# Moving the inverse's remainder products between the two parts of the forward transform, in a fused FFT convolution and expert kernel

## The chip, the cores and the metric

One core of a Trainium2 chip runs the whole kernel. The metric is the device time of one execution in microseconds (us). Engines are called PE (TensorE), DVE (VectorE), ACT (ScalarE), POOL (GpSimd) and SP (SyncE, which here issues DMAs only).

## The reference

A long convolution along the sequence, with a filter that a small network makes, is followed by a mixture of experts with one expert a token:

```
h_filt = (max(pos_emb @ w1, 0) @ w2) * exp(-0.01 * pos)         # 10048 x 128
u = x * v                                                       # 4 x 10048 x 128
y = irfft(rfft(u, 2S) * rfft(h_filt, 2S), 2S)[:, :S]            # along the sequence
xy = x * y
group, expert = first maximum of xy @ w_group, of xy @ w_expert[group]
out[token] = gate * max(xy @ w1[group, expert], 0) @ w2[group, expert]
```

## The kernel before, in words

The sequence is seen as 79 blocks of 128 positions, and each transform of length 2 x 10048 is done in two steps by matrix products: along the blocks (157 points, of which 79 frequencies are kept, real and imaginary), then along the positions within a block. All values are 32-bit.

`conv` makes the filter's spectrum, then runs over the four batches in five rounds, which are called **ways** here (loop `b` at L275). In way b the forward transform of batch b and the inverse of batch b - 1 go together; way 0 has no inverse, way 4 no forward transform. Ways 1, 2 and 3 are the **combined ways**. The first part of a way runs over the 128 channels in 22 tiles (`OUTS`: twenty of 6 channels, two of 4), taken as eleven **pairs**; the second part, the **middle**, runs over the 79 frequencies, multiplies by the filter's spectrum (`middle`, L595, L778 to L782) and transforms back along the positions (`back`, L791), while the tokens of batch b - 1 are routed (`chosen`, L955 and on).

For one pair of a combined way the program has, in this order:

- `turned` (L810, L813 on PE, L815 on ACT): twelve channels of the previous batch's spectrum `z`, and the rest of them in `zr`, are transposed into four PSUM buffers `pt`, and ACT copies each of these to an SBUF tile `tt`. The first copy holds the transposed rest.
- `dft_main`, twice (L462): the forward products of 64 of the block rows, one tile of 6 channels after the other. They use a 64x64 form of PE's array, four of them side by side. Each tile has two accumulators `psa`. Those of the pair's first tile come out of pool `psA` (2 buffers), those of the second out of pool `psT` (4 buffers), from which the `pt` of `turned` come too.
- `dft_rest`, for both tiles at once (L477 with 32 rows, L487 with 16): the forward products of the remaining block rows, added to the four accumulators. Its last four products end all four. `dft_leave` (L505) then copies each accumulator out: the part up to frequency 63 to `z` by ACT, the remainder to `zr` by DVE.
- `inverse_rest` (L825): the inverse's products with the rest of the frequencies, again in the 64x64 form, from `tt` number one into the two accumulators `po` of the pair (pool `psO`, 2 buffers).
- `inverse_blocks`, twice (L846): the inverse's other products, with 128 rows, added to `po`, tile by tile. ACT copies and turns a half of each `po` into `oo` (L855, L856), DVE adds (L860, `yt`) and multiplies by x (L862, `xy`).

On PE, ACT and DVE these instructions stand in the order in which a scheduler put the program's calls; each engine works through its own list and waits, where the next instruction waits. ACT's list for a steady pair is: four z copies (L505), L855, L856, L855, L856, four tt copies (L815).

Pool and buffer of the forward accumulators are chosen here:

```
pool, tag = (self.psT, "pt") if ((d0 + 2) // GI % (2 if b else 3)) else (self.psA, "ps")
pss = [pool.tile([128, GD, 2 * NB], F32, tag=tag, name="psa") for _ in HALVES]
```

Of the kernel before, what the change touches and what calls it, by code (L numbers as in the profile page):

```python
# [141 lines left out]
def columns(wide):  # L142
    return -(-NB // wide) * (wide + 1)


def groups(n, step):
    return [(i, min(step, n - i)) for i in range(0, n, step)]
# [15 lines left out]
class Kernel:  # L163
# [67 lines left out]
    def conv(self, ctx, right):  # L231
        tc, nc, d = self.tc, self.nc, self.d
        cp = ctx.enter_context(tc.tile_pool(name="cconst", bufs=1))
        zp = ctx.enter_context(tc.tile_pool(name="z", bufs=1))
        self.psA = ctx.enter_context(tc.tile_pool(name="psA", bufs=2, space=PSUM, reuse_waits="tile"))
        self.psT = ctx.enter_context(tc.tile_pool(name="psT", bufs=4, space=PSUM, reuse_waits="tile"))
        banks = ctx.enter_context(ExitStack())
        open_bank = lambda name, n: banks.enter_context(
            tc.tile_pool(name=name, bufs=n, space=PSUM, reuse_waits="tile")
        )  # L240
        self.psO = open_bank("psO", 2)
        self.psr = lambda shape, name: self.psL.tile(shape, F32, tag="pl", name=name)
        self.fmr = self.rp.tile([128, 2 * NCG * 20], F32, tag="fmr", name="fmr")
        self.fm = self.fmr[:, : 4 * NB].rearrange("p (h k) -> p h k", h=2)
        self.fr = self.fmr[:, 4 * NB : 12 * NB].rearrange("p (h c k) -> p h c k", h=2, c=2)

        self.z = zp.tile([128, D, KM, 2], F32, name="z")
        self.zr = zp.tile([128, D, 16, 2], F32, name="zr")
        nc.vector.memset(self.zr[:, :, NB - KM :], 0.0)
        ahead = ExitStack()  # L250
        made, folded, self.loads = [], [], []
        first = ExitStack()
        self.hp = first.enter_context(tc.tile_pool(name="head", bufs=NHEAD))
        with ExitStack() as c2:
            self.filter(c2, ahead, folded)
        for j in range(0, len(OUTS), 2):
            self.dft_rest(0, [self.dft_main(*folded[i]) for i in (j, j + 1)])
            while len(folded) < min(len(OUTS), NFIRST + 3 + j // 2, max(NFIRST, j + 2) + NPROD):
                engine = (nc.vector, nc.gpsimd)[len(folded) % 2]
                folded.append(self.fold(*self.product(0, *OUTS[len(folded)], engine), engine))  # L260
                self.load_next(folded)
        first.close()
        folded = []
        bp = ctx.enter_context(tc.tile_pool(name="back", bufs=1))
        self.fi = bp.tile([128, 2, 3, NB], F32, name="fi")
        nc.sync.dma_start(self.fi.rearrange("p h a t -> p (h a t)"), d["c_fi"])


        xyp = ctx.enter_context(tc.tile_pool(name="xy", bufs=1, reuse_waits="tile"))
        inner = ExitStack()  # L270
        self.sp = inner.enter_context(tc.tile_pool(name="stream", bufs=2, reuse_waits="tile"))
        routing, self.scatters = iter(()), []

        self.anchor, self.loose = None, []
        for b in range(self.nbat + 1):  # L275
            last = b == self.nbat
            if last:
                ahead.close()
                inner.close()
                self.sp = ctx.enter_context(tc.tile_pool(name="stream", bufs=2, reuse_waits="tile"))  # L280
                weights = self.first_weights(right)
            if b > 0:
                xy = xyp.tile([128, NB, D], F32, tag="xy", name=f"xy{b - 1}")
            if b == 1:
                self.router_consts()
            for j, (d0, n) in enumerate(OUTS if b else []):
                if j % 2 == 0:
                    tts = self.turned(d0, min(2 * GI, D - d0), last)
                if not last and j % 2 == 0:
                    units = []  # L290
                    for i in range(j, j + 2):
                        self.run_ahead(b, i, made, folded)
                        self.scatter(1)
                        units.append(self.dft_main(*folded[i]))
                    self.dft_rest(b, units)
                if j % 2 == 0:
                    pos = self.inverse_rest(min(2 * GI, D - d0), tts)
                self.inverse_blocks(b - 1, xy, d0, n, tts, pos[j % 2], j % 2)
                if not last:
                    self.scatter(1 + j % 2)  # L300
                if last:
                    next(weights, None)
                    if j == 16:
                        self.scatter(sum(1 for s in self.scatters if s[0] < self.nbat - 2))
                        self.all[0].load(self.rows)
                for _ in range(3 if last else 1):
                    next(routing, None)
                if last:
                    self.scatter(1 + j % 2)
            made, folded = [], []  # L310
            if b > 0:
                rp = self.rp
                banks.close()
                self.psL = open_bank("psL", 2 if last else 1)
                m = NCG + 1
                shape = [128, columns(m - 1) // m, NE, m]
                oh = rp.tile(shape, F32, tag="oh", name="oh")
                en = self.entries.tile([128, NB, 2], F32, tag="en", name="en")
                pos = rp.tile([*shape[:2], m], F32, tag="pos", name="pos")
                cnt = rp.tile([128, NE], F32, tag="cnt", name="cnt")  # L320
                if not last:
                    self.scratch = self.psL.tile([128, 512], F32, tag="work", name="work")
                args = b - 1, xy, oh, en, pos, cnt
                routing = chain(self.chosen(*args), self.ranked(b - 1, *args[2:]))
                stored = 0
                if last:
                    self.identr = self.rows.tile([128, 128], F32R, name="identr")
                    nc.scalar.copy(self.identr, self.ident)
                    for i in range(CHOSEN):
                        if i == 3:  # L330
                            self.all[0].prepare(self.rows, self.psA)
                        next(routing)
            if not last:
                back = []
                for i, (k0, n) in enumerate(groups(NB, 2)):
                    back.append(self.middle(b, k0, n))
                    if len(back) > LAG:
                        self.back(*back.pop(0))
                    if b == 1 and i == 1:
                        self.clear_none()  # L340
                    self.scatter(i % 4 // 3, False)
                    while b > 0 and stored < min(len(groups(NB, 4)), (i + 2) * 20 // STORES):
                        self.store(b - 1, xy, stored)
                        stored += 1
                    next(routing, None)
                for i in range(-AHEAD - 1, 0):
                    self.run_ahead(b + 1, i, made, folded)
                for args in back:
                    self.back(*args)
                for _ in routing:  # L350
                    pass
                if b > 0:
                    banks.close()
                    self.psO = open_bank("psO", 2)
        return routing
# [1383 lines left out]
```

## Time and profile before

| | us |
|---|---|
| runs: median (lowest to highest) | 1792.52 (1791.48 to 1794.69) |
| profiled execution: its time | 1792.42 |
| profiled execution: its span in the trace | 1790.2 |
| PE busy | 1745.2 |
| DVE busy | 1362.4 |
| ACT busy | 1211.5 |
| POOL busy | 1007.6 |

The span is the time from the first to the last instruction of the trace; the 2.2 us to the execution's time lie around it. Busy times are sums over the span. Lines are those of the kernel before. In the trace every 32-bit product shows as two passes of PE, so that the 12 products of L825 in a pair are 24 rows of the trace; a merged row gives their count as x24.

### The profile page before, as it was taken

Reading aid. Unit: us, or ns where it says so; the run is one execution under the profiler, and the core shown is the slowest. Engines: PE = TensorE matmul, PEld = TensorE weight load, DVE = VectorE, ACT = ScalarE, POOL = GpSimd, SP = SyncE. Lnnn points to the kernel's source line nnn. Section 1 sums busy time; section 2 is a strip of 40 time slices with the busy share of each in tenths; the row PEclk is TensorE's granted clock in tenths of the full one; section 3 lists DMA queues with packets and bytes.
Section 4 is the critical chain, followed back from the end, with each engine's and each line's share of the span. In section 5 each row is a group of like instructions: output and inputs, shape, how many; then the busy total and the mean of one; then the engine's idle time right before and its main releaser. Section 6 shows DMA issues by size and latency. Waiting matters only on the chain.

```text
span 1790.2 us, 44965 instructions
## 1 busy us (share of the span) xinstructions
PE 1745.2 (97%) x15302; PEld 1471.2 (82%) x15302; DVE 1362.4 (76%) x3048; ACT 1211.5 (68%) x2624; POOL 1007.6 (56%) x1147
## 2 busy tenths in 40 slices
PE   8999999999999999999999999999999999999998
PEld 7977888878787878777888788888888888889998
DVE  5587777797689768845888898777777777778886
ACT  6573377537654765466777777777777777778886
POOL 4526801577867776784566657766764333333454
PEclk9999999999999999999999999999999999999999
DMA  5697976989898999668633434344443333223342
GB/s 176 224 339 231 306 220 212 324 264 291 290 320 262 288 300 312 222 202 276 210 115 117 126 119 161 126 140 141 138 128 92 92 93 95 88 78 103 96 126 93
DMA packets 201327, 337.30 MB, mean 188 GB/s; under 512 B 26856, under 2 KB 88525, under 8 KB 201088
## 3 DMA queue, kind: packets, MB, share of 16 engines
q1 hardware_dynamic: 170304, 274.57, 48.0%
q0 software_dynamic: 21280, 44.23, 7.0%
q10 hardware_dynamic: 9504, 15.54, 3.0%
q8 instruction: 123, 2.02, 0.5%
q14 instruction: 116, 0.95, 0.2%
HBM read 259.27 MB, written 75.53 MB: 187 GB/s over the span
## 4 chain that ended last, share of the span: by engine, by line
PE 54%; ACT 1%; issue 1%; DVE 1%; DMA 0%; SPq 0%; POOL 0%; DVEq 0%; ACTq 0%; POOLq 0%
PE ph L1550 8%; PE ph L1552 8%; PE py L1572 8%; PE ph L1551 8%; PE py L1570 8%; PE py L1571 8%; PE ptm L1584 2%; PE px L1501 1%; PE po L825 1%; PE po L846 1%; PE ptr L955 0%; ACT oo L856 0%; ACT hh L1558 0%; DMA xo<-x_out 0%; ACT tt L815 0%
## 5 line engine op out<-in xcount | busy, mean ns | idle before, releaser
L1559 DVE SCALAR_TENSOR_TENSOR hl<-ph,hh 128x512 fp32r<-128x512 f32 (+1 forms) x656 | 440.0, 672 | 136.1 <-ACT hh L1558 131.1
L1596 POOL DMA_INDIRECT out<-os,to x320 | 323.4, 1011 | 385.4 <-ACT os L1591 313.0
L1558 ACT ACTIVATE hh<-ph 128x512 fp32r<-128x512 f32 (+1 forms) x656 | 388.8, 593 | 169.1 <-PE ph L1552 139.9
L429 POOL DMA_INDIRECT prow<-stg,adr x316 | 327.5, 1036 | 104.6 <-issue 67.0
L1550 PE MATMUL ph<-xh,wh 128*128 128x512 f32 (+2 forms) x720 | 278.1, 386 | 1.0 <-ACT wh L1529 1.0
L1552 PE MATMUL ph<-xh,wl 128*128 128x512 f32 (+2 forms) x720 | 264.5, 367 | 0.2 <-DVE wl L1539 0.2
L1572 PE MATMUL py<-hh,wl 128*128 128x512 f32 (+2 forms) x720 | 264.3, 367 | 0.0
L1570 PE MATMUL py<-hh,wh 128*128 128x512 f32 (+2 forms) x720 | 264.2, 367 | 0.0
L1551 PE MATMUL ph<-xl,wh 128*128 128x512 f32 (+2 forms) x720 | 263.6, 366 | 0.0
L1571 PE MATMUL py<-hl,wh 128*128 128x512 f32 (+2 forms) x720 | 263.2, 366 | 0.0
L779 POOL TENSOR_TENSOR y<-t 128x256 f32<-128x256 f32 (+1 forms) x160 | 119.5, 747 | 157.8 <-DVE t L778 150.1
L798 ACT COPY z<-pbp 128x512 f32<-128x512 f32 x128 | 75.0, 586 | 140.6 <-PE pbp L791 140.4
L791 PE MATMUL pbp<-y,bp 128*128 128x256 f32 x632 | 161.9, 379 | 3.7 <-POOL y L782 3.6
L595 PE MATMUL psb<-z,bt 128*128 128x256 f32 x640 | 161.2, 380 | 3.4 <-PE psb L595 1.4
L1571 PEld LDWEIGHTS py<-hl,wh 128*128 128x128 f32 x720 | 135.7, 188 | 22.6 <-DVE hl L1559 0.6
L1552 PEld LDWEIGHTS ph<-xh,wl 128*128 128x128 f32 x720 | 135.4, 188 | 22.2 <-DVE wl L1539 0.4
L1572 PEld LDWEIGHTS py<-hh,wl 128*128 128x128 f32 x720 | 135.6, 188 | 21.6
L1570 PEld LDWEIGHTS py<-hh,wh 128*128 128x128 f32 x720 | 135.5, 188 | 21.5
L1550 PEld LDWEIGHTS ph<-xh,wh 128*128 128x128 f32 x720 | 135.5, 188 | 16.7 <-ACT wh L1529 1.2
L1551 PEld LDWEIGHTS ph<-xl,wh 128*128 128x128 f32 x720 | 136.0, 189 | 15.8
L778 DVE TENSOR_TENSOR t<-psb,ht 128x512 f32<-128x512 f32 (+1 forms) x160 | 108.6, 679 | 43.1 <-POOL y L779 13.9
L791 PEld LDWEIGHTS pbp<-y,bp 128*128 128x128 f32 x632 | 117.7, 188 | 25.4 <-POOL y L782 8.0
(270 smaller groups left out, 3367.6 us busy)
## 6 DMA issues: line engine op xcount, KB each, us to landing
ws<-m_w SPq DMA_DIRECT2D x178, 256.0 KB
xv<-xv_in SPq DMA_DIRECT2D x80, 512.0 KB
ht<-hspec SPq DMA_DIRECT2D x156, 256.0 KB
bt<-c_b SPq DMA_DIRECT2D x95, 256.0 KB
bp<-c_bp SPq DMA_DIRECT2D x76, 256.0 KB
xyd<-xy SPq DMA_DIRECT2D x76, 256.0 KB
stg<-xyd SPq DMA_DIRECT2D x76, 256.0 KB
xg<-prow SPq DMA_DIRECT2D x66, 260.0 KB
```

Of the source, the lines that this page charges most:

```text
L429: ins = self.nc.gpsimd.indirect_dma_start(self.d["prow"], bass.IndirectOffsetOnAxis(ap=u.adr[:, t + t // u.wide + 1 : t + t // u.wide + 2] ...
L595: nc.tensor.matmul(ps[:, i].rearrange("p s d -> p d s"), bt[:, i], self.frequency(k0 + i, 1)[:, :, 0], start=True, stop=True,)
L791: nc.tensor.matmul(by_part[:, i], bp[:, i], y[:, i], start=True, stop=True,)
L1550: k.fix(nc.tensor.matmul(ph[:, j], wh, self.xh, start=True, stop=False))
L1551: k.fix(nc.tensor.matmul(ph[:, j], wh, self.xl, start=False, stop=False))
L1552: k.fix(nc.tensor.matmul(ph[:, j], wl, self.xh, start=False, stop=True))
L1558: k.fix(nc.scalar.activation(hh, ph, AF.Relu))
L1559: k.fix(nc.vector.scalar_tensor_tensor(hl, ph, 0.0, hh.bitcast(F32), ALU.max, ALU.subtract))
L1570: k.fix(nc.tensor.matmul(self.py, wh, hh, start=(c == 0), stop=False))
L1571: k.fix(nc.tensor.matmul(self.py, wh, hl, start=False, stop=False))
L1572: k.fix(nc.tensor.matmul(self.py, wl, hh, start=False, stop=(c == NC - 1)))
L1596: ins = k.nc.gpsimd.indirect_dma_start(k.d["out"], bass.IndirectOffsetOnAxis(ap=self.to[:, h : h + 1], axis=0), o, None, bounds_check=k.nt ...
```

## The change

Inside a combined way, `inverse_rest` of a pair is called ahead of `dft_rest` of the same pair.

```
                         units.append(self.dft_main(*folded[i]))
-                    self.dft_rest(b, units)
                 if j % 2 == 0:
                     pos = self.inverse_rest(min(2 * GI, D - d0), tts)
+                    if not last:
+                        self.dft_rest(b, units)
                 self.inverse_blocks(b - 1, xy, d0, n, tts, pos[j % 2], j % 2)
```

The line numbers behind it grow by one (L825 becomes L826, and so on). On PE, a steady pair of way 1 before (psa are the forward accumulators, po the inverse's, pt the transposes):

```order
L810 MATMUL pt<-ident,zr 128x128 x3
L813 MATMUL pt<-ident,z 128x128 x12
L462 MATMUL psa<-fmr,eo 64x158 x24
L477 MATMUL psa<-fmr,eo 64x316 x8
L487 MATMUL psa<-fmr,eo 64x158 x8
L825 MATMUL po<-fi,tt 64x158 x12
L846 MATMUL po<-fi,tt 64x79 x24
```

The same pair on PE in the changed kernel:

```order
L811 MATMUL pt<-ident,zr 128x128 x3
L814 MATMUL pt<-ident,z 128x128 x12
L463 MATMUL psa<-fmr,eo 64x158 x24
L826 MATMUL po<-fi,tt 64x158 x12
L478 MATMUL psa<-fmr,eo 64x316 x8
L488 MATMUL psa<-fmr,eo 64x158 x8
L847 MATMUL po<-fi,tt 64x79 x24
```

The twelve products of `inverse_rest` moved from behind the forward rest to the place right behind the forward main; nothing else moved on PE within a pair. The 33 pairs all change in this way, but for the first of way 3, where five of the twelve already stood ahead of L462.

On ACT, the list of a steady pair in the changed kernel, from the z copies on (its order is that of before, with lines one higher):

```order
L506 COPY z<-psa 128x384 x4
L856 ACTIVATE oo<-po 64x474
L857 COPY oo<-po 64x474
L856 ACTIVATE oo<-po 64x474
L857 COPY oo<-po 64x474
L816 COPY tt<-pt 128x384
L816 COPY tt<-pt 128x512 x3
```

The z copies wait for the end of the forward rest on PE, and L856 and all that follows stand behind them.

On DVE, where way 1 goes over into its middle stage, before (yt and xy are the inverse's last steps, psb the first product of the middle, t its product with the spectrum):

```order
L860 TENSOR_TENSOR yt<-po,oo 128x316
L862 TENSOR_TENSOR xy_3007<-yt,xo 128x79x4
L860 TENSOR_TENSOR yt<-po,oo 128x316
L778 TENSOR_TENSOR t_4587<-psb,ht 128x512
L862 TENSOR_TENSOR xy_3007<-yt,xo 128x79x4
L781 TENSOR_TENSOR t_4590<-psb,ht 128x512
```

And in the changed kernel:

```order
L861 TENSOR_TENSOR yt<-po,oo 128x316
L779 TENSOR_TENSOR t_4587<-psb,ht 128x512
L863 TENSOR_TENSOR xy_3007<-yt,xo 128x79x4
L861 TENSOR_TENSOR yt<-po,oo 128x316
L782 TENSOR_TENSOR t_4590<-psb,ht 128x512
L863 TENSOR_TENSOR xy_3007<-yt,xo 128x79x4
```

The last product of xy, on which the router's transposes wait, now has two spectrum products ahead of it where it had one. POOL's list is the same; on SP some loads of the middle stage (`ht`, `bt`, `bp`) change places with each other and with the stores of `xy`.

## Rows read from the trace of the kernel before

**Rows 1.** The page: busy time by engine, and PE's granted clock in 40 slices

```profile
PE 1745.2 (97%) x15302; PEld 1471.2 (82%) x15302; DVE 1362.4 (76%) x3048; ACT 1211.5 (68%) x2624; POOL 1007.6 (56%) x1147
...
PEclk9999999999999999999999999999999999999999
```

**Rows 2.** Timeline of PE, way 1, first pair: start us, duration us, instructions

```profile
225.72 1.84 PE L462 MATMUL psa<-fmr,eo 64*64 64x158 f32 x48
227.49 0.79 PE L477 MATMUL psa<-fmr,eo 32*64 32x316 f32 x16
228.07 0.47 PE L487 MATMUL psa<-fmr,eo 16*64 16x158 f32 x16
```

**Rows 3.** Timeline of PE, way 1, fourth pair

```profile
247.72 1.91 PE L462 MATMUL psa<-fmr,eo 64*64 64x158 f32 x48
249.56 0.79 PE L477 MATMUL psa<-fmr,eo 32*64 32x316 f32 x16
250.14 0.47 PE L487 MATMUL psa<-fmr,eo 16*64 16x158 f32 x16
250.55 1.04 PE L825 MATMUL po<-fi,tt 64*64 64x158 f32 x24
251.51 1.86 PE L846 MATMUL po<-fi,tt 128*64 128x79 f32 x48
```

**Rows 4.** Timeline of ACT, fourth and fifth pair; in brackets idle time before, and releaser

```profile
247.58 0.97 ACT L815 COPY tt<-pt 128x384 f32<-128x384 f32 x2
...
250.68 1.63 ACT L505 COPY z<-psa 128x384 f32<-128x384 f32 x4 [1.15 <-PE psa L487]
...
252.66 0.56 ACT L855 ACTIVATE oo<-po 64x474 f32<-64x474 f32 x1 [0.36 <-PE po L846]
...
254.96 0.48 ACT L815 COPY tt<-pt 128x384 f32<-128x384 f32 x1
```

**Rows 5.** Timeline of PE: L487 of pair ten (way 1), one and ten (ways 2, 3)

```profile
294.39 0.48 PE L487 MATMUL psa<-fmr,eo 16*64 16x158 f32 x16
...
400.52 0.47 PE L487 MATMUL psa<-fmr,eo 16*64 16x158 f32 x16
...
467.25 0.47 PE L487 MATMUL psa<-fmr,eo 16*64 16x158 f32 x16
...
576.70 0.47 PE L487 MATMUL psa<-fmr,eo 16*64 16x158 f32 x16
...
643.88 0.47 PE L487 MATMUL psa<-fmr,eo 16*64 16x158 f32 x16
```

**Rows 6.** Timeline, end of way 1's pairs and start of its middle stage

```profile
299.21 1.35 ACT L815 COPY tt<-pt 128x256 f32<-128x256 f32 x3
...
300.32 0.79 PE L477 MATMUL psa<-fmr,eo 32*64 32x316 f32 x16
...
301.04 0.77 PE L825 MATMUL po<-fi,tt 64*64 64x158 f32 x16
301.17 1.20 ACT L505 COPY z<-psa 128x256 f32<-128x256 f32 x4 [0.61 <-PE psa L477]
...
301.74 1.32 PE L846 MATMUL po<-fi,tt 128*64 128x79 f32 x32
...
302.55 0.43 ACT L855 ACTIVATE oo<-po 64x316 f32<-64x316 f32 x1 [0.18 <-PE po L846]
...
302.98 2.00 PE L595 MATMUL psb<-z,bt 128*128 128x256 f32 x8
...
303.44 0.49 DVE L860 TENSOR_TENSOR yt<-po,oo 128x316 f32<-128x316 f32 x1 [0.82 <-ACT oo L856]
...
304.77 0.68 DVE L778 TENSOR_TENSOR t<-psb,ht 128x512 f32<-128x512 f32 x1
...
305.90 1.09 PE L955 MATMUL ptr<-ident,xy 128*128 128x128 f32 x8 [0.91 <-DVE xy L862]
```

**Rows 7.** Timeline of PE, way 2, third group of the middle stage's products

```profile
483.95 1.11 PE L595 MATMUL psb<-z,bt 128*128 128x256 f32 x4 [0.78 <-PE psb L595]
```

More of the change, by code (lines that the diff above doesn't have):

```diff
@@ L294, in conv @@
                         units.append(self.dft_main(*folded[i]))
-                    self.dft_rest(b, units)
                 if j % 2 == 0:
                     pos = self.inverse_rest(min(2 * GI, D - d0), tts)
+                    if not last:
+                        self.dft_rest(b, units)
                 self.inverse_blocks(b - 1, xy, d0, n, tts, pos[j % 2], j % 2)
```

## The prediction

> **What bounds the kernel now.** I read the page first: TensorE is busy in 97% of the span, at the upper of its two clock levels in all 40 slices [rows 1]. So what adds a wait on PE adds to the time. The change is in the three combined ways alone (b = 1, 2, 3; eleven tile pairs each), so the next view is the timeline of PE there.
>
> The first pair of way 1 runs with PE alone as its limit: the forward main (L462) takes 225.72 to 227.49, 1.77 us [rows 2]. In a steady pair it takes 247.72 to 249.56, 1.84 us [rows 3]. Something holds PE for 0.07 us, and the rows of ACT in the same stretch show what. ACT ends its second copy of transposed data (L815, two copies from 247.58) at 248.55 [rows 4], about half-way through L462, where the second tile of the pair begins. That tile's two accumulators come out of pool psT, whose four buffers also hold the transposes; by the program's waits its first products wait for the first and second L815 copy of the same pair. PE is at its limit and ACT's chain just reaches it.
>
> The reader should see a ring, each step started by the end of the one before. Second L815 copy ends, to L477: 1.01. L477 to L487: 0.58. L487 to L825: 0.41. L825 to L846: 0.96 [rows 3]. L846's first half to ACT's first L855: 1.15, and that row says that ACT waited 0.36 for L846. L855, L856, L855, L856 and up to L815: 2.30 (252.66 to 254.96). Two L815 copies: 0.97 [rows 4]. Sum 7.38, which is the pair's period (247.58 to 254.96). In the same ring stands a second branch, now idle: L487 releases the z copies (L505), 0.54 after its start, and they keep ACT for 1.63 [rows 3, 4]. They are done at 252.31, 0.35 before L846 lets ACT go on. That 0.35 is what the change spends.
>
> **Part 1: the moved products.** Per pair the same instructions run; L825 now follows L462, which uses the same 64x64 tiles, and L477 follows L825. What does it save? 24 passes of L825 take 0.96 [rows 3], the 16 passes of the last pair 301.04 to 301.74, 0.70 [rows 6]. Eight passes are 0.26, so 24 are 0.79 without the change of tile form around them, and 0.17 goes with entering and leaving the form. One such change falls away: 33 x 0.17 = 5.6 us of PE time. Bounds: nothing saved (L825 still 0.96), or twice the 0.17, if entering and leaving each cost that much.
>
> The Trainium skill (TensorEngine Tiling, Tiling Modes, Key Properties) says that a change of tiling mode, unlike a change of tile, drains TensorE. The trace agrees with 0.17 us; by that rule alone the change is a gain, and this is the first rival below.
>
> **Part 2: what is moved behind it.** The forward rest (L477, L487) starts 0.79 later relative to L462. It completes all four accumulators of the pair, so all four z copies leave 0.79 later. ACT's order of instructions is the same before and after: z copies, then L855, L856 twice, then the L815 copies. The 0.35 of room is used up and the other branch closes the ring: second L815 copy ends, to L477 1.01 + 0.79 = 1.80; to L487 0.58; to the z copies 0.54; z copies 1.63 and 0.02 to the next; L855 to L815 2.30; two copies 0.97. Sum 7.84, against 7.38 now. PE's own work would allow 7.38 - 0.07 - 0.17 = 7.14, so PE gets a stall of 0.70 in the middle of L462 in each pair but the first of a way. The gain of part 1 is off the path: it only lengthens that stall.
>
> L487 of pair 1 to L487 of pair 10 in way 1 is 228.07 to 294.39, 66.32 [rows 2, 5]; nine rounds of 7.84 are 70.56: +4.2. L487 of pair 1 is itself 0.79 late. Bounds of one round: 7.14 (the copies don't hold PE) and 8.0 (L825 costs its full 0.96).
>
> **Part 3: the end of a way.** From L487 of pair 10 to the first transposes for the router (L955) is 294.39 to 305.90, 11.51 [rows 5, 6]. Afterwards: z copies and up to L855 0.54 + 1.63 + 0.02 = 2.19; to the first L815 +2.30 = 4.49; from there to L477 1.11 (299.21 to 300.32), plus L825 at 0.70 - 0.17 = 0.53, gives 6.13; the last z copies start 0.85 later (300.32 to 301.17) and take 1.20: 8.18. The middle stage's first product (L595) now waits for them too, where it was free at 302.98. L855 at 8.20; L860 0.89 later (302.55 to 303.44): 9.09; L860 to L955 2.46. The order on DVE changes here: a second spectrum product (L781) comes ahead of the last product of xy, on which L955 waits. It costs at most the 0.68 of its sister L778; I take 0.5, as L778, moved between L860 and the L862 that needs it, covers some of a wait there. That is 12.05: +0.5. Bounds 0 and 0.9, the wait that L955 has now.
>
> SP's queue also changes its order where the ways hand over (loads of bt, ht and bp against the stores of xy). No row shows PE waiting for one of these; I take 0, between -0.9 and +0.9 a way, again the wait of L955 [rows 6]. POOL's order does not change; its row scatters run in the longer pairs. PE may get back the 0.78 that it waits early in way 2's middle stage [rows 7], since POOL, which is behind there with scatters, has more time.
>
> **Sum.** Way 1: 0.8 + 4.2 + 0.5 = 5.5. Way 2: the same span is 400.52 to 467.25, 66.73 [rows 5], 0.4 longer for a stop of PE within the ring, which stays; 5.5 - 0.8 = 4.7. Way 3: 576.70 to 643.88, 67.18 [rows 5], 0.9 longer; such stops vanish where they fall into the new stall, so I count half as absorbed, and five of the twelve moved products of its first pair already stood ahead of L462: 4.8. Together 15.0. Everything behind is a chain on PE and shifts. The profiled execution took 1792.42, the median is 1792.52: 1792.4 + 15.0 = 1807.4.
>
> **The rivals.** (a) *The form change is all that counts.* If the copies don't hold PE, the 5.6 us come through, less 3 x 0.5 at the ends: 1788.3. For it: PE is busy in 97%, and the 0.17 that a change of form costs shows in every pair. Against it: L462 at 1.84 against 1.77, and a period that equals the ring's sum to 0.01. It decides where the z copies end before L846's first half does: counted from L487 that is 0.54 + 1.63 = 2.17 against 0.41 + 1.15 = 1.56 with L846 right behind it, so the copies would have to take under 1.0. Chance 0.07.
> (b) *No change*, within 3.6 us: PE gets back in the middle stages most of what the pairs lose, as DVE and POOL, and not PE, pace their ends. For it: waits like that of rows 7. Against: one such wait a way, below 1 us each. 1794; chance 0.05.
> (c) *More than the ring*: the order of SP's loads adds a wait at each hand-over, or the new stall brings the clock down. With 0.9 a way twice over 3 ways it is 1813. PE now has waits of 0.9 at upper clock [rows 1, 6], longer than the new 0.70, so I give the clock little. Chance 0.06.
> The Trainium skill (TensorE: Matmul & The Clock Gate, "A second HAM failure mode: psum-queue depth-cycling") reports short idles between groups, from cycling through PSUM buffers, that made the clock swing. At the lower level PE's 2.9 us of the ring would double, some 87 us over 30 pairs; no row here shows such a fall.
>
> **How the numbers follow.** The ring as forecast has 0.82, and 1807.4 is its value. Its own spread: the end of a way 0 to 0.9 and SP's 0.9 either way make about 4 us, the absorbed stops and the wait of rows 7 another 2. Low end 1801, high end 1812.5; (a), (b) and the far part of (c) are left out. 0.2% is 3.6 us, about what a measurement of this kernel tells from no change: faster 0.07, same 0.05, slower 0.88.
>
> **What would show it.** Right: from the second pair of each way L463 (L462 before) lasts about 2.4 us, with PE waiting for tt of L816; periods of 7.84; L826 at 0.79; ACT's wait ahead of L856 gone and that ahead of the z copies longer, near 1.9 instead of 1.15. Wrong: periods of 7.2 (rival a), or L826 still at 0.96 (part 1).

## The result and the profile after

| | before | after |
|---|---|---|
| median (lowest to highest), us | 1792.46 (1791.1 to 1794.69) | 1807.99 (1806.63 to 1810.82) |
| profiled execution's span, us | 1790.2 | 1804.7 |

The ratio is 1.0089, 95% interval [1.0077, 1.0101]: the change costs 15.5 us. The forecast was 1807.4, in 1801.0 to 1812.5.

Some experiments below ran on other chips, on which PE pauses again and again for nothing that the trace shows and the kernel before itself takes some 2047 to 2050 us; their times are compared only with that, and their readings are taken from way 1, whose pairs show no such pauses: the four kernels that ran on both kinds of chip agree in way 1's length within 0.02 us.

The page of the changed kernel, busy time and PE's granted clock:

```profile
PE 1757.7 (97%) x15302; PEld 1474.4 (82%) x15302; DVE 1366.7 (76%) x3048; ACT 1211.7 (67%) x2624; POOL 1008.7 (56%) x1147
...
PEclk9999999999999999998999999999999999999999
```

ACT, DVE and POOL run as many instructions as in [rows 1]. PE's busy time grew by 12.5 us with the same 15302 instructions: while PE waits in a forward main, single passes of L463 run where four run side by side otherwise, and the page counts that time as busy. The one slice with an 8 lies at 812 to 857 us, behind the combined ways. The kernel before was granted the same 0.89 in the stretch that answers to it, 797 to 842; there the fall lies across the border of two slices, and both still show a 9, so the row of nines in [rows 1] hides some 10 us at the lower level. Over the combined ways the granted clock is 1.00 in both kernels, so the clock is no part of the difference.

Timeline of PE, first pair of way 1 in the changed kernel (start, duration, instructions), which answers to [rows 2]:

```profile
225.61 1.84 PE L463 MATMUL psa<-fmr,eo 64*64 64x158 f32 x48
227.27 0.98 PE L826 MATMUL po<-fi,tt 64*64 64x158 f32 x24
228.18 0.79 PE L478 MATMUL psa<-fmr,eo 32*64 32x316 f32 x16
228.77 0.48 PE L488 MATMUL psa<-fmr,eo 16*64 16x158 f32 x16
```

Where nothing holds PE, the new order is the better one: L463 to L826 takes 1.66 where L462 to L477 took 1.77, and L826 to L478 takes 0.91 where L825 to L846 took 0.96 in a steady pair. The first pair as a whole takes 7.14 from its first transpose to the next pair's, against 7.30 before.

The same view, fourth pair, which answers to [rows 3]:

```profile
248.50 2.41 PE L463 MATMUL psa<-fmr,eo 64*64 64x158 f32 x45
250.63 0.29 PE L826 MATMUL po<-fi,tt 64*64 64x158 f32 x1
250.74 0.31 PE L463 MATMUL psa<-fmr,eo 64*64 64x158 f32 x3
250.76 1.09 PE L826 MATMUL po<-fi,tt 64*64 64x158 f32 x23
251.78 0.79 PE L478 MATMUL psa<-fmr,eo 32*64 32x316 f32 x16
252.37 0.48 PE L488 MATMUL psa<-fmr,eo 16*64 16x158 f32 x16
252.77 1.86 PE L847 MATMUL po<-fi,tt 128*64 128x79 f32 x48
```

From L463 to L478 it is 3.28 here and 2.57 in the first pair: 0.71 of waiting, all within L463. PE's weight loads (PEld) there show what is waited for, and the last line, PEld's waits over all three combined ways (us in total, times, longest), shows it as the longest wait in the list, about 0.6 us in each of 30 pairs; the kernel before has no wait of L462 on `tt` in its list:

```profile
249.53 0.19 PEld L463 LDWEIGHTS psa<-fmr,eo 64*64 64x64 f32 x2 [0.29 <-ACT tt L816]
250.02 0.60 PEld L463 LDWEIGHTS psa<-fmr,eo 64*64 64x64 f32 x19 [0.30 <-ACT tt L816]
...
PEld psa L463 <- ACT tt L816: 18.4, 57, 0.8
```

Timeline of ACT there, which answers to [rows 4] (in brackets idle time before, and releaser):

```profile
249.00 0.48 ACT L816 COPY tt<-pt 128x384 f32<-128x384 f32 x1
...
249.38 1.57 ACT L816 COPY tt<-pt 128x512 f32<-128x512 f32 x3
...
252.90 1.63 ACT L506 COPY z<-psa 128x384 f32<-128x384 f32 x4 [1.95 <-PE psa L488]
254.55 0.57 ACT L856 ACTIVATE oo<-po 64x474 f32<-64x474 f32 x1
...
256.85 0.48 ACT L816 COPY tt<-pt 128x384 f32<-128x384 f32 x1
```

The period is 256.85 - 249.00 = 7.85. The bracket has moved: before, ACT waited 1.15 ahead of the z copies and 0.36 more ahead of L855; now it waits 1.95 ahead of the z copies and not at all behind them. The z copies close the ring.

L488 of pair ten (way 1), and of pairs one and ten (ways 2 and 3), which answer to [rows 5]:

```profile
299.46 0.48 PE L488 MATMUL psa<-fmr,eo 16*64 16x158 f32 x16
...
406.72 0.48 PE L488 MATMUL psa<-fmr,eo 16*64 16x158 f32 x16
...
477.41 0.47 PE L488 MATMUL psa<-fmr,eo 16*64 16x158 f32 x16
...
587.01 0.47 PE L488 MATMUL psa<-fmr,eo 16*64 16x158 f32 x16
...
657.71 0.47 PE L488 MATMUL psa<-fmr,eo 16*64 16x158 f32 x16
```

Nine rounds now take 70.69, 70.69 and 70.70 in the three ways, where they took 66.32, 66.73 and 67.18: every pair now goes at the ring's pace, and the short stops of before are gone in it.

End of way 1's pairs and start of its middle stage, PE, ACT and DVE, which answers to [rows 6]:

```profile
304.37 0.63 PE L463 MATMUL psa<-fmr,eo 64*64 64x158 f32 x11 [0.45 <-ACT tt L816]
...
306.44 1.20 ACT L506 COPY z<-psa 128x256 f32<-128x256 f32 x4 [1.15 <-PE psa L478]
...
307.69 2.00 PE L596 MATMUL psb<-z,bt 128*128 128x256 f32 x8
...
308.55 0.49 DVE L861 TENSOR_TENSOR yt<-po,oo 128x316 f32<-128x316 f32 x1 [0.66 <-ACT oo L857]
...
310.35 0.68 DVE L782 TENSOR_TENSOR t<-psb,ht 128x512 f32<-128x512 f32 x1
...
310.94 0.47 DVE L863 TENSOR_TENSOR xy<-yt,xo 128x316 f32<-128x316 f32 x1
...
311.13 0.67 PE L596 MATMUL psb<-z,bt 128*128 128x256 f32 x2 [1.44 <-issue]
...
311.64 1.03 PE L956 MATMUL ptr<-ident,xy 128*128 128x128 f32 x8
```

L782 stands ahead of the last L863 as the order on DVE said, and PE waits 1.44 where it waited 0.91. The profile names no releaser ("issue"); that it is L782, done at 311.03, is read from the times. But then one more product of the middle stage (L596, 0.51 until L956) comes first, so part of that wait is not lost.

Where the 14.5 us of the span lie, from the first transpose row (L810, now L811) of each stretch: the ten rounds up to the last pair grew by 4.21, 3.80 and 3.08 us in ways 1, 2 and 3 (73.63 to 77.84, 74.03 to 77.83, 76.34 to 79.42). From the last pair to the next way's first pair it is +1.30, +0.58 and +1.40 (98.82 to 100.12, 100.30 to 100.88, 99.28 to 100.68). All that lies behind, 1043.91 before, is 1044.15.

### The profile page after: what moved, and what is told of

Its sections match the earlier page's. It is cut to its first block, busy times and chain, and to the rows that moved or that the text cites. A ratio compares the mean times of both kernels' runs of the same rounds, so it can differ in the third digit from the quotient of the medians.

```text
span 1804.7 us, 44966 instructions
## 1 busy us (share of the span) xinstructions
PE 1757.7 (97%) x15302; PEld 1474.4 (82%) x15302; DVE 1366.7 (76%) x3048; ACT 1211.7 (67%) x2624; POOL 1008.7 (56%) x1147
## 4 chain that ended last, share of the span: by engine, by line
PE 54%; ACT 1%; issue 1%; DVE 1%; DMA 0%; POOL 0%; DVEq 0%; SPq 0%; ACTq 0%; POOLq 0%
PE ph L1551 8%; PE ph L1553 8%; PE py L1573 8%; PE ph L1552 8%; PE py L1571 8%; PE py L1572 8%; PE ptm L1585 2%; PE px L1502 1%; PE ptr L956 1%; PE po L826 1%; PE po L847 0%; PE plt L967 0%; ACT oo L857 0%; ACT tt L816 0%; DMA xo<-x_out 0%
## 5 line engine op out<-in xcount | busy, mean ns | idle before, releaser
L596 PE MATMUL psb<-z,bt 128*128 128x256 f32 x640 | 161.9, 381 | 7.2 <-issue 4.3
L596 PEld LDWEIGHTS psb<-z,bt 128*128 128x128 f32 x640 | 115.4, 188 | 28.6 <-issue 6.9
```

Of the source, the lines that this page charges most:

```text
L596: nc.tensor.matmul(ps[:, i].rearrange("p s d -> p d s"), bt[:, i], self.frequency(k0 + i, 1)[:, :, 0], start=True, stop=True,)
```

## The experiments

**The theory**: ACT's copies close the ring; PE's stall is what ACT's list takes too long. **The rival**: PE itself pays for the new order, ACT's waits only follow. They part when ACT's list alone is made longer or shorter. **A second question** is how much belongs to the last pairs. One table holds the readings: the start of the first transpose of pairs 2 and 10 of way 1, an eighth of the difference (the mean period), and the time from the last pair to way 2's first pair.

| kernel | pair 2 | pair 10 | period | last pair to way 2 |
|---|---|---|---|---|
| before | 231.23 | 290.18 | 7.37 | 98.82 |
| after | 230.96 | 293.81 | 7.86 | 100.12 |
| before, small copy more | 233.67 | 294.74 | 7.63 | 99.49 |
| before, two copies more | 232.17 | 294.97 | 7.85 | 99.79 |
| change in last pairs only | 231.33 | 290.27 | 7.37 | 99.50 |
| change but for last pairs | 230.93 | 293.76 | 7.85 | 99.46 |
| before, two copies off ACT | 230.57 | 289.00 | 7.30 | 98.65 |
| change, one copy off ACT | 232.04 | 291.83 | 7.47 | 99.86 |
| change, two copies off ACT | 231.88 | 289.03 | 7.14 | 99.95 |
| the same, last pairs in the old order | 231.01 | 288.15 | 7.14 | 98.67 |

### ACT made slower in the kernel before

The old order on PE is kept; only ACT gets more to do behind the z copies. First a small copy, a repeat of 128 columns:

```diff
         for _, d0, m, pss in units:
             self.dft_leave(b, d0, m, pss)
+        for _ in range(1 if b else 0):
+            ins = nc.scalar.copy(
+                self.z[:, d0 + m : d0 + m + 1].rearrange("p d k s -> p d (k s)"), pss[1][:, :1, : 2 * KM]
+            )
...
```

> The kernel before, with one copy repeated on ACT behind the z copies of each pair of the combined ways: 128 columns of the second tile's second accumulator once more to the same place, about 0.17 us of ACT per pair (from L505's 0.48 for 384 columns and the 0.11 that 128 columns more or fewer change an ACT copy). Ring theory: the z branch has 0.35 of room before L846's first half, so the period stays 7.38 and the time 1792.5, within 1. Rival, ACT's load itself is what counts (every us of ACT in a pair adds to the pair): 33 x 0.17 = 5.6 more, 1798.

Measured: 2048.35 us, ratio 1.0019 [0.9995, 1.0043], which tells nothing on that chip; the period is 7.63. Timeline of ACT:

```profile
261.61 1.63 ACT L512 COPY z<-psa 128x384 f32<-128x384 f32 x4 [1.15 <-PE psa L487]
263.55 0.27 ACT L491 COPY z<-psa 128x128 f32<-128x128 f32 x1 [0.32 <-DVE zr L512]
263.84 0.56 ACT L862 ACTIVATE oo<-po 64x474 f32<-64x474 f32 x1
```

I had missed on the dose: the repeat takes 0.27, not 0.17, and waits 0.32 for DVE's copy of the remainder. From the end of the z copies (261.61 + 1.63) to L862 it is 0.60, 0.58 more than the usual 0.02. The room is 0.35, so 0.23 should come through, 7.38 + 0.23 = 7.61. The expectation failed and the ring holds, but that reading was made afterwards, so the next run is the test. Here the z copies of the second accumulators are made twice:

```diff
+        for _, d0, m, pss in units if b else ():
+            ins = nc.scalar.copy(self.z[:, d0 + m : d0 + 2 * m].rearrange("p d k s -> p d (k s)"), pss[1][:, :m, : 2 * KM])
...
```

> The kernel before, with the z copies of the second accumulator of each tile done twice, 0.37 each, 0.75 us of ACT more behind the z copies of each pair. Ring theory: 0.35 is covered, 0.40 is not; period 7.38 + 0.40 = 7.78 from the second pair on, 9 x 0.41 a way and some 0.4 at its end, 3 x 4.1 = 12 more: 1804.5. Rival, ACT's load counts in full: 33 x 0.75 = 25 more, 1817. Rival, the form of PE's tiles alone sets the pairs: no change, 1792.5.

Measured: 2055.65 us, ratio 1.0040 [1.0015, 1.0066]; period 7.85. From the first z copy to L860 it is now 263.43 - 260.98 = 2.45, where it is 1.63 [rows 4] and the 0.02 to the next instruction:

```profile
260.98 1.63 ACT L510 COPY z<-psa 128x384 f32<-128x384 f32 x4 [1.15 <-PE psa L487]
262.47 0.94 ACT L491 COPY z<-psa 128x384 f32<-128x384 f32 x2
263.43 0.56 ACT L860 ACTIVATE oo<-po 64x474 f32<-64x474 f32 x1
```

That is 0.80 more (0.75 were expected), less the room of 0.35: 0.45, and 7.38 + 0.45 = 7.83, against 7.85; ACT's load in full would have given 8.18. So the old order, with 0.80 us more on ACT, takes the period that the new order takes with its z copies 0.8 later.

### ACT made faster

Two copies of each steady pair go to DVE: the first tt copy and the z copy of the second tile's second accumulator. The same edit goes into the kernel before and into the changed one:

```diff
             if b == 0:
                 copies = (copies[r],) * 2
+            elif r == 1 and (d0 + 2) // GI % 2:
+                copies = (nc.vector.tensor_copy,) * 2
...
-            (nc.vector.tensor_copy if other and len(tts) == 2 else nc.scalar.copy)(tt[:, :m], pt[:, :m])
+            (nc.vector.tensor_copy if (other and len(tts) == 2) or (not other and s is None) else nc.scalar.copy)(tt[:, :m], pt[:, :m])
```

> The kernel before, with two copies of each steady pair taken off ACT and put on DVE: the first tt copy (L815, 128x384) and the z copy of the second tile's second accumulator (L505). Theory (the ring closed by ACT's copies): ACT's chain in the pair gets shorter than PE's own work, so the period of way 1 falls from 7.37 to PE's own 7.30 (its first pair), and nothing below that: 33 x 0.07 = 2 us less, ratio to before 0.999. Rival (the copies do not hold PE; PE pays for the order itself): the period stays at 7.37, ratio 1.000, or above it if the copies on DVE are in the way of its own work.

> The changed kernel with the same two copies on DVE. Theory (ring): ACT no longer closes the ring, the stall in the forward main goes, and the period of way 1 falls from 7.85 to PE's own 7.14 as in the first pair; 30 pairs x 0.71 = 21 us less than the changed kernel, about 1.5 to 4 us below the kernel before with the same two copies (one change of tile form a pair saved, 0.16 each, less what the ends of the ways cost); ratio to before about 0.997. Rival (PE itself pays for the new order): the period stays near 7.85 and the ratio to before at 1.009.

Measured periods: 7.30 and 7.14, both as the theory had them. Both times, 2055.47 and 2056.45, have the ratio 1.0042 ([1.0017, 1.0068] and [1.0016, 1.0068]): on that chip both kernels are slower than the kernel before, and what ways 2 and 3 add there stays open. A steady pair of the changed kernel with the two copies on DVE, from its second run, PE:

```profile
247.74 1.84 PE L463 MATMUL psa<-fmr,eo 64*64 64x158 f32 x48
249.40 0.98 PE L828 MATMUL po<-fi,tt 64*64 64x158 f32 x24
250.32 0.79 PE L478 MATMUL psa<-fmr,eo 32*64 32x316 f32 x16
250.90 0.47 PE L488 MATMUL psa<-fmr,eo 16*64 16x158 f32 x16
251.31 1.86 PE L849 MATMUL po<-fi,tt 128*64 128x79 f32 x48
```

and of the kernel before with them:

```profile
246.66 1.84 PE L462 MATMUL psa<-fmr,eo 64*64 64x158 f32 x48
248.44 0.79 PE L477 MATMUL psa<-fmr,eo 32*64 32x316 f32 x16
249.02 0.48 PE L487 MATMUL psa<-fmr,eo 16*64 16x158 f32 x16
249.42 1.04 PE L827 MATMUL po<-fi,tt 64*64 64x158 f32 x24
250.39 1.86 PE L848 MATMUL po<-fi,tt 128*64 128x79 f32 x48
```

L463 to L849 takes 3.57, L462 to L848 takes 3.73: the 0.16 of one change of form less. In the first the forward main goes through in 1.66, with no stall, although L478 and L488 still come behind L828 and the z copies still leave late. So the new order alone costs PE nothing; it costs what ACT adds. The rival is out.

One copy alone, the first tt copy, on DVE in the changed kernel (the second of the two hunks above):

> The changed kernel with one copy alone on DVE, the first tt copy (L816, 128x384). Theory (ring): 0.4 to 0.5 us come out of the ring, and part of the stall stays: period of way 1 7.40 to 7.50 instead of 7.85, 30 x 0.4 = 12 us less than the changed kernel, ratio to before about 1.002. Rival (PE itself pays): 7.85 and 1.009.

Measured: period 7.47, in the range expected; 2054.36 us, ratio 1.0028 [1.0001, 1.0055]. The dose answers in steps: 7.86 with both copies on ACT, 7.47 with one less, 7.14 with two less, where PE's own work is the limit.

### The last pairs

The change in all pairs but the last of a way, and the reverse:

```diff
+                    if j == 20:
+                        self.dft_rest(b, units)
                 if j % 2 == 0:
                     pos = self.inverse_rest(min(2 * GI, D - d0), tts)
-                    if not last:
+                    if not last and j < 20:
                         self.dft_rest(b, units)
```

> The changed kernel, but the last pair of each combined way keeps the order of before (forward rest, then the inverse's rest), and with it DVE keeps its order at the hand-over. Ring theory: pairs 2 to 10 still take 7.85; at the end of the way 0.6 to 0.7 less than in the changed kernel, so 2 us less, 1806. Rival, most of the loss sits at the hand-overs: the loss falls to a third or less, under 1798.

> The kernel before, with the change in the last pair of each combined way alone. Ring theory: pairs 1 to 10 keep 7.30 to 7.38; at the end of a way the z copies are 0.5 late and DVE has one product more ahead of the last xy, L955 0.5 to 0.9 later, in way 2 won back by the wait that PE has anyway: 1794.5. Rival, most of the loss sits at the hand-overs: 1800 or more.

Measured: 2047.18 (0.9998 [0.9970, 1.0027]) and 2050.55 (1.0009 [0.9984, 1.0033]), both useless as times. In way 1 the first has the ring's period and 0.64 more from the last pair on than the kernel before; the second has the old period and 0.68 more. Together 1.32, against the 1.30 of the whole change: half of the hand-over's loss is the last pair's own order, half is the lateness that the ring has already brought (in the first of the two, PE still waits for `tt` in the last pair's forward main, which takes 2.15 to L480, 302.85 to 305.00, against 1.52 in the kernel before).

> The change in the last pair of each combined way alone, once more for its time over all three ways; in the trace of its first run way 1 was 0.66 us longer than in the kernel before. Theory (the last pair and its hand-over are a small share): 3 x 0.7 = 2 us, 1795, ratio 1.0011. Rival (a third or more of the change's 15.5 us comes from the hand-overs, as way 1's stretch from the last pair to the router's transposes grows by 1.0 to 1.6): 1798 or more, ratio above 1.0025.

Measured: 1793.01 us, ratio 1.0003 [0.9994, 1.0012], so between 1.1 less and 2.2 more than the kernel before. The 2 us of the theory are just inside, the 5 us of the rival are not: the loss is in the pairs.

### Back to whole times

Three kernels of the above, on chips on which the kernel before takes 1793:

> The changed kernel with the two copies on DVE, once more for its time over all three ways. Way 1 took 171.38 us in the trace of its first run, against 172.45 in the kernel before and 177.95 in the changed one. Theory (ring): 3 x 1.07 = 3.2 us less than the kernel before: 1789.3, ratio 0.998; against the changed kernel 18.7 less. Rival (PE itself pays for the new order, and way 1 was an exception): 1800 or more, ratio above 1.004. [...]

> The kernel before with the two copies on DVE, once more for its time over all three ways, as the partner of the changed kernel with the same copies, which took 1791.7 here (1787.9 with the last pairs in the old order). Way 1 took 171.69 us in the trace of its first run, against 172.45 in the kernel before. Theory (ring): without ACT in the way the new order of the ten full pairs is worth 0.16 a pair, so this kernel is about 30 x 0.16 = 5 us above the one with the last pairs old: 1791 to 1793, ratio 0.999 to 1.000. Rival (the gain of that kernel comes from the copies on DVE, and the new order is worth nothing): 1788, ratio 0.997.

Measured: 1791.70 (0.9989 [0.9981, 0.9998]) with the change, 1790.49 (0.9991 [0.9982, 1.0000]) without it. Two copies on DVE take back 16.3 of the changed kernel's us, 1807.99 to 1791.70; 18.7 were expected. With them on DVE the change moves the time by 1.2 us (on two chips, and within the noise of the two ratios), where it cost 15.5. That settles the cause of the loss over all three ways. But the change's gain does not show in these two times: way 1 is 171.40 against 171.70, and way 2 is 174.80 against 173.01.

The remaining candidate keeps the old order in the last pairs:

> As the one before, with the last pair of each combined way in the order of before. Theory: the pairs at 7.14 as there; at the end of a way the z copies leave as in the kernel before, so the stretch from the last pair to the router's first transposes is shorter than there by up to 0.9 us a way: up to 2.7 us less, ratio to before about 0.996. Rival (the end of a way costs nothing once ACT has room): the same time as the one before, within 1 us.

> The changed kernel with the two copies on DVE and the last pairs in the order of before, once more for its time over all three ways. In the trace of its first run way 1 took 170.10 us from the first pair to the next way's first pair, against 172.45 in the kernel before. Theory (ring): the same 2.4 us in each of three ways, 7 us in all: about 1785.5 us on a chip on which the kernel before takes 1792.5, ratio 0.996. Rival (ways 2 and 3 give it back in the middle stages, since DVE, which has two more copies a pair, paces them): 1790 to 1792, ratio 0.999 to 1.000. [...]

Measured in the first run 2051.18 (1.0012 [0.9984, 1.0040]), with way 1 at 170.10; in the second 1787.92 us, ratio 0.9973 [0.9963, 0.9982]. **This version beats both kernels**, the one before by 5 us (0.27%; 7 were expected) and the changed one by 20; on the chip of the first run there is no difference. It is 2.6 below the kernel before with the same two copies, where 5 were expected. These two ran on different chips, and their intervals touch (0.9963 to 0.9982, and 0.9982 to 1.0000), so the gain of the order alone is weakly shown as a time; in way 1 it is 1.6 us, 170.12 against 171.70, ten pairs at 0.16. Ways 2 and 3 gain less than way 1, and its trace shows stops there, PE:

```profile
425.28 0.84 PE L851 MATMUL po<-fi,tt 128*64 128x79 f32 x18 [0.54 <-issue]
...
431.92 0.50 PE L490 MATMUL psa<-fmr,eo 16*64 16x158 f32 x9 [0.48 <-issue]
...
630.24 0.63 PE L851 MATMUL po<-fi,tt 128*64 128x79 f32 x12 [1.45 <-issue]
```

PE pauses in the midst of a group, for nothing that the profile shows. Way 2's pairs take 73.59 here, against 71.43 in way 1; the kernel before with the two copies has 73.03 in both. The pauses are not all of it: way 3's stretch from the last pair on takes 99.98, against 99.28 in the kernel before. And this profiled execution took 1790.73, 2.8 more than the median. Whether the pauses come with the faster pairs or fall so by chance can't be told from one profiled execution of each; no run was made for it.

## Why the prediction was right

**What bounds the kernel.** Right. The ring's sum was forecast as 7.84; the rows of after have 7.85. Its terms: second L816 copy ends (249.00 + 0.97) to L478 1.81, forecast 1.80; to L488 0.59 (0.58); to the z copies 0.53 (0.54); to L856 1.65 (1.65); to L816 2.30 (2.30); two copies 0.97. The runs that slow and relieve ACT show that it is a cause and not only a sum that fits.

**Part 1, the moved products.** Right in size, wrong in place. Forecast: one change of form is 0.17, and it would show as L826 at 0.79. Measured: 0.16 a pair (7.30 to 7.14, in the first pairs and in all with the copies off ACT), but 0.11 of it stands in the forward main, 1.77 to 1.66, and 0.05 in the moved products, 0.96 to 0.91. By these rows most of the cost stands in the group that leaves the 64x64 form, and L826 still leaves it. In a stalled pair L826 takes even 1.02 (250.76 to 251.78), so the sign that was named, 0.79 if right and 0.96 if wrong, was no test of it; the period was. The Trainium skill (TensorEngine Tiling (Array Packing), Tiling Modes, Key Properties) says that a change of mode drains TensorE; the 0.16 agrees, and it is all that the rule is worth here.

**Part 2, what is moved behind.** Right: nine rounds 70.69 against 70.56, a stall of 0.71 against 0.70, L488 of pair one 0.81 later in its pair (228.77 - 223.82 against 228.07 - 223.93), forecast 0.79. ACT's wait ahead of L856 is gone, and that ahead of the z copies is 1.95, forecast near 1.9.

**Part 3, the end of a way.** Right, with a small miss. L488 of pair ten to L956 is 311.64 - 299.46 = 12.18, forecast 12.05, from 11.51. Not foreseen was that an L596 would slip in ahead of L956, so that not all of it is lost: way 1 as a whole is 5.51 longer (4.21 + 1.30), forecast 5.5. The wait of 0.78 in way 2 [rows 7] is gone, and way 2's middle grew by 0.58 where way 1's grew by 1.30, so the 0.7 that this was to give back did come back. Way 2 as a whole is 4.39 longer, forecast 4.7, and way 3 4.48, forecast 4.8: **the mis-sized term** is how many stops of PE the new stall absorbs. I let the 0.4 of way 2 stay and took half of way 3's 0.9; the rounds of 70.69 and 70.70 show that all went. SP's changed order cost PE nothing that shows. The sum was 15.0; the two profiled executions differ by 14.2 (1806.63 against 1792.42), the medians by 15.5. That the median came within 0.6 us of the forecast is in part luck.

**The rivals.** (a) fell by its own condition: the z copies would have had to take under 1.0 and take 1.63; with two copies off ACT its premise holds, and then the pairs do run at the 7.14 that PE alone allows. (b) fell: the middles got longer, not shorter. (c) fell: PE waits for none of the reordered loads (DVE waits 2.12 us for one `ht`, at 498.48 in way 2, and no stop of PE follows), and the clock kept its upper level. The Trainium skill's report of a swinging clock (TensorE: Matmul & The Clock Gate, "A second HAM failure mode: psum-queue depth-cycling") is not borne out by this run: 0.71 of waiting for a PSUM buffer in each of 30 pairs left every slice of the combined ways at 9. On the other chips, where PE's pauses are shorter and far more frequent, the clock does fall (last section).

## What to carry to other kernels

Before moving work on the busiest engine, add up the loop that runs through the engine that looks idle: if one branch of it has 0.35 us of room and the move delays it by 0.8, the difference is paid in every round, whatever the move saves. The saving is not lost for good; it waits until the other engine has been given room, and two small edits (two copies moved to DVE, the last pairs left as they were) made a loss of 15.5 us into a gain of 5, of which the two copies alone give about 2 in the kernel before (1792.71 to 1790.49, at the edge of the noise). Here the ring showed as a bracket that stands ahead of one instruction of ACT's loop, the first z copy, and of no other.

## What was not expected of the hardware

In each stalled pair, L826's first pass starts ahead of the forward main's last three: at 250.63, with the three passes of L463 from 250.74 on. In PE's list all of L463 stands ahead of L826 (but for the first pair of way 3). In the first pairs of ways 1 and 2, with no wait, no L826 starts before L463's last, so the overlap comes with the wait: two passes go on at 249.53, ahead of all the others at 250.02 (PEld above), and that lead is still there at the end of the group. The Trainium skill (TensorEngine Tiling (Array Packing), Tiling Modes, Key Properties) says that different tiles can load weights and multiply in parallel; the rows agree, by 0.11 us in a pair.

On the other chips the same program pauses from way 2 on. Changed kernel with two copies on DVE, first run, PE:

```profile
423.39 0.49 PE L828 MATMUL po<-fi,tt 64*64 64x158 f32 x3 [0.22 <-issue]
424.11 0.52 PE L828 MATMUL po<-fi,tt 64*64 64x158 f32 x4 [0.23 <-issue]
424.85 0.48 PE L828 MATMUL po<-fi,tt 64*64 64x158 f32 x3 [0.23 <-issue]
```

Three or four passes, then 0.23 us of nothing, again and again: most pairs there take 10 to 14 us instead of 7 to 8. The granted clock falls too: it is 1.00 in way 1, 0.95 in way 2 and 0.93 in way 3, against 1.00 in all three in the second run of the same kernel. Ways 2 and 3 take 222.03 and 223.82 us, against 174.80 and 175.15, and the larger part of the loss lies behind them (1205.7 against 1044.1, clock 0.96). Whether the pauses bring the clock down isn't shown. What PE waits for the profile does not name, and no run was made on it. It cost eight of the twelve runs their times, and way 1, where it does not happen, kept their readings usable.
